# Attention outputs turned by DMA transposes of two f16 halves instead of fp32 TensorE transposes, from the second batch on

## The chip, the cores and the metric

One core of a Trainium2 chip runs the whole program. The metric is device microseconds of one execution. Engines are written as in the profile: PE is TensorE's matmul side and PEld its weight load, DVE is VectorE, ACT ScalarE, POOL GpSimd, and SP SyncE, which issues every DMA of this kernel.

## The reference

There are B = 8 batches of H = 8 heads, with S = 1152 keys and D = 64. Queries are averaged in pairs, so a head has TQ = 576 of them. The attention result, with the heads side by side, is the input x of a channel mix:

```python
q_pool = q.reshape(B, H, S // 2, 2, D).mean(axis=3)
scores = q_pool @ k.T / sqrt(D)
attn   = exp(scores - max);  attn /= attn.sum(-1) + 1e-9
x      = (attn @ v).transpose(0, 2, 1, 3).reshape(B, 576, 512)

x_prev = x shifted by one token, zeros first
xk, xr = mu_k * x + (1 - mu_k) * x_prev,  mu_r * x + (1 - mu_r) * x_prev
out    = sigmoid(xr @ w_r) * (relu(xk @ w_k) ** 2 @ w_v)
```

## The kernel before, in words

**Tiling.** The 64 heads are counted by n. Each is worked in six blocks of QN = 96 queries (`block`): first-pass scores (L479, nine matmuls of 128x96), a maximum over keys on DVE (L486), a small matmul that turns it (L489), a second maximum (L492), a small matmul that spreads it (L494), an ACT instruction that writes it into a row of the query tile (L497), second-pass scores (L503), and the exponential on ACT (L509), which leaves the packed weights `pf`. POOL takes their low parts out into `pl` (L512). Three PSUM tiles `s0` to `s2` rotate over the blocks. Keys and values of the next head are split into f16 pairs by `prep`: `kr` is loaded, ACT and POOL make `kn` (L430, L435), and a DMA transpose on SP's queue turns it into `ks1` (L438), nine blocks of 128x128 in one instruction. Queries of a pair of heads go the same way through `qn` (L397) and a DMA transpose to `qT` (L413).

**The place of the change.** `window` multiplies weights with values (L538, L540, L545) into the one PSUM tile `a`. A head has five windows, the first of 64 queries and four of 128. After the last of them ACT copies the first window's low part across (L562), DVE adds it (L564), and the result is divided into `xb` (L566 to L569), a single fp32 buffer of [128 queries, 5 windows, 2 heads, 64]. When the second head of a pair is there (hh = 1), five fp32 transposes on PE (L581), three and then two, turn `xb` by windows back into `a`, and ACT copies each part into `xt` (L584): `xt` is [128 features of the pair, 4 pairs, 1 + 576 tokens] in fp32, one of three buffers by batch. The transposes and the copies therefore stand between a pair and the next head's first window, which writes the same tile `a`. There are 32 pairs.

**The channel mix.** `ff` works tiles of 256 tokens, 18 in all, as soon as the batch that holds their last token is done. `mix` forms xk and xr from `xt` (ACT L653, DVE L656), rounds (ACT L662) and takes the rest on POOL (L664); the products are on PE (L684) with three f16 terms for each, ACT squares (L711, L713), POOL splits (L715), and so on to the output. Since a tile sums over all 512 features, it needs all four pairs of its batch. The three tiles that need batch 7 are left when attention ends; for the last batch the products take turns in five PSUM tiles, so that the first 8 of the 24 terms of each of four of them can run ahead.

**Weights.** `weights` loads 20 pieces through the two staging tiles `st0` and `st1` (4 KB a partition each) and splits them into f16 pairs on ACT, DVE and POOL; this is done while the first batches run.

**The order.** Nothing is issued when it is written. Every step is recorded by `op(engine, cost, function, r=, w=, key=)` with a cost in microseconds, what it reads and writes, and a key; `Issue.run` simulates several list schedules from these costs and fixed latencies, takes the one that comes out shortest, and issues every engine's instructions in that order. The order on each engine is then fixed; at run time an instruction waits only for the semaphores of what it needs, with everything behind it on its engine or queue. A cost in an `op` call is thus no work, but it moves the order. A step marked `port` (every POOL step, and a DVE step so marked) is kept apart from others so marked in the simulation.

Of the kernel before, what the change touches and what calls it, by code (L numbers as in the profile page):

```python
# [12 lines left out]
F16 = mybir.dt.float16  # L13
# [3 lines left out]
AF = mybir.ActivationFunctionType  # L17
# [3 lines left out]
P = 128  # L21
# [237 lines left out]
def kernel(  # L259
# [40 lines left out]
    def bufs(name, n, shape, dt):  # L300
        return [const.tile(shape, dt, name=f"{name}{i}") for i in range(n)]
# [43 lines left out]
    r32, tmp = bufs("r32", 2, [P, 2, T], F32), bufs("tmp", 2, [P, T], F32)  # L345
    ex, em = (bufs(n, 2, [P, DM], F32) for n in ("ex", "em"))
    st = bufs("st", 2, [P, 1024], I32)
    whi, wlo = {}, {}
    for n, w, kc in (("k", w_k, NG), ("v", w_v, NF), ("r", w_r, NG)):
        whi[n] = const.tile([P, kc, w.shape[1]], F16, name=f"w{n}_hi")  # L350
# [108 lines left out]
    def block(n, j, i, t):  # L459

        hp, z = n % 2, i % 3
        qi = n // 2 % 2
        q0 = hp * TQ + j * QN
        qhi, qlo = (qT[qi][:, r].rearrange("p j x -> p (j x)")[:, q0:q0 + QN] for r in (0, 1))
        kh, kl = ([(t_, qi, hp, j, j0) for j0, j1 in ((0, 5), (5, NQ)) if q0 < j1 * P and q0 + QN > j0 * P]
                  for t_ in ("qT", "qTl"))
        s = s_b[z]
        rows = slice(j * QN, (j + 1) * QN)
        mxz, mbz = mx[z], mb[z]

        def cols(c0, c1):
            return s[:, P + c0 * QN:P + c1 * QN]

        def grid(c0, c1):
            return cols(c0, c1).rearrange("p (c q) -> p c q", q=QN)

        def scores(c0, c1):
            for c in range(c0, c1):
                nc.tensor.matmul(cols(c, c + 1), ks1[hp][:, c, :], qhi,  # L479
                                 start=(c == c0), stop=False, skip_group_check=True)  # L480

        for c0, c1 in BK:
            op("PE", (c1 - c0) * 0.043, lambda c0=c0, c1=c1: scores(c0, c1),
               r=[("ks1", hp, c) for c in (0, 5) if c < c1 and (c0 < 5 or c)] + kh, w=[("s", z)], key=t)

        op("DVE", 0.967, lambda: nc.vector.tensor_reduce(mxz, grid(0, NC).rearrange("p c q -> p q c"),  # L486
                                                         axis=AX.X, op=ALU.max),
           r=[("s", z)], w=[("mx", z)], key=t)
        op("PE", 0.054, lambda: nc.tensor.matmul(s[0:QN, 0:P], mxz, identb, start=False, stop=False,  # L489
                                                 skip_group_check=True),  # L490
           r=[("mx", z)], w=[("s", z)], key=t + O_MAX)
        op("DVE", 0.199, lambda: nc.vector.tensor_reduce(mbz[0:QN], s[0:QN, 0:P], axis=AX.X, op=ALU.max),  # L492
           r=[("s", z)], w=[("mb", z)], key=t + O_MAX)
        op("PE", 0.05, lambda: nc.tensor.matmul(s[:, 0:QN], mbz[0:QN].broadcast_to([QN, P]),  # L494
                                                 negi[0:QN, 0:QN], start=False, stop=False, skip_group_check=True),
           r=[("mb", z)], w=[("s", z)], key=t + O_MAX)
        op("ACT", 0.133, lambda: nc.scalar.activation(qlo[QN:QN + 1], s[QN:QN + 1, 0:QN], AF.Prelu,  # L497
                                                      scale=1.0 - EPS, alpha=(1.0 + EPS) / (1.0 - EPS)),
           r=[("s", z)] + kl, w=kl, key=t + O_MAX)

        def scores2(c0, c1):
            for c in range(c0, c1):
                nc.tensor.matmul(cols(c, c + 1), ks2[hp][:, c, :], qlo,  # L503
                                 start=False, stop=True, skip_group_check=True)

        for c0, c1 in BK:
            op("PE", (c1 - c0) * 0.043, lambda c0=c0, c1=c1: scores2(c0, c1),
               r=[("ks2", hp)] + kl, w=[("s", z)], key=t + O_EXP)
        op("ACT", NC * QN / 1200 + 0.051, lambda: nc.scalar.activation(  # L509
            pf[:, :, HALF + rows.start:HALF + rows.stop], grid(0, NC), AF.Exp, bias=SHIFT, scale=0.125 / (2.0 * SQ)), r=[("s", z)], w=[("pf", j)], key=t + O_EXP)  # L510
        def lows(to, r0, r1, buf):
            op("POOL", NC * (r1 - r0) / 1000 + 0.066, lambda: nc.gpsimd.tensor_scalar(  # L512
                to, half(pf, U16, 0)[:, :, HALF + r0:HALF + r1], LO, 1.0, op0=ALU.mult, op1=ALU.mult),
               r=[("pf", j)], w=[buf], key=t + O_REST)

        r0 = rows.start
        if j == 0:
            lows(half(pf, F16, 1)[:, :, 0:HALF], 0, HALF, ("pside",))
            r0 = HALF
        lows(pl[:, :, r0:rows.stop], r0, rows.stop, ("pl", j))  # L520

    def window(n, w, t):


        b, h = divmod(n, H)
        g, hh = divmod(h, 2)
        r0, size, _ = WIN[w]
        side = size < P
        jv = n % NV
        VN = D + 1  # L530
        vk = [(x, jv, c0) for x in ("vt", "vtl") for c0 in (0, 5)]
        js = range(r0 // QN, (r0 + size - 1) // QN + 1)
        a0, rows = w * VN, slice(r0, r0 + P)
        his = slice(0, P) if side else slice(HALF + r0, HALF + r0 + P)

        def hi(c0, c1):
            for c in range(c0, c1):
                nc.tensor.matmul(a_b[:, a0:a0 + VN], half(pf, F16, 1)[:, c, his], vt[jv][:, c, D:D + VN],  # L538
                                 start=(w == 0 and c == 0), stop=False, skip_group_check=True)
                nc.tensor.matmul(a_b[:, a0:a0 + D], half(pf, F16, 1)[:, c, his], vt[jv][:, c, 0:D],  # L540
                                 start=False, stop=(side and c == NC - 1), skip_group_check=True)

        def lo(c0, c1):
            for c in range(c0, c1):
                nc.tensor.matmul(a_b[:, a0:a0 + VN], pl[:, c, rows], vb[jv][:, c, 0:VN],  # L545
                                 start=False, stop=(c == NC - 1), skip_group_check=True)

        for c0 in (0, 3, 6):
            op("PE", 3 * 0.0595, lambda c0=c0: hi(c0, c0 + 3),
               r=vk + [("pf", j) for j in js] + ([("pside",)] if side else []) + ([("a",)] if c0 or w else []),  # L550
               w=[("a",)], key=t)
        for c0, c1 in () if side else ((0, 5), (5, NC)):
            op("PE", (c1 - c0) * 0.030, lambda c0=c0, c1=c1: lo(c0, c1),
               r=[("vb", jv)] + [("pl", j) for j in js] + [("a",)], w=[("a",)], key=t)
        if w < NW - 1:
            return

        u = a_b[:, 0:NW * VN].rearrange("p (k x) -> p k x", k=NW)
        z = n % 2
        dz, xz = den[z], xb[0]  # L560
        up = slice(HALF, P)
        op("ACT", 0.25, lambda: nc.scalar.activation(cross[up], a_b[0:HALF, 0:VN], AF.Copy, scale=VLO),  # L562
           r=[("a",)], w=[("cross",)], key=t + O_EVAC)
        op("DVE", 0.16, lambda: nc.vector.tensor_tensor(a_b[up, 0:VN], a_b[up, 0:VN], cross[up], op=ALU.add),  # L564
           r=[("cross",), ("a",)], w=[("a",)], key=t + O_EVAC)
        op("DVE", 0.075, lambda: nc.vector.tensor_scalar(dz, u[:, :, D], GUARD, None, op0=ALU.add),  # L566
           r=[("a",)], w=[("den", z)], key=t + O_EVAC)
        op("DVE", 0.08, lambda: nc.vector.reciprocal(dz, dz), r=[("den", z)], w=[("den", z)], key=t + O_EVAC)
        op("DVE", 0.07 + NW * D / 960, lambda: nc.vector.tensor_tensor(  # L569
            xz[:, :, hh], u[:, :, 0:D], dz.unsqueeze(2).broadcast_to([P, NW, D]), op=ALU.mult),  # L570
           r=[("den", z), ("a",)], w=[("xb", hh)], key=t + O_EVAC)
        if hh == 0:
            return
        for k0, k1 in TURN:
            q0, qe = spans(k0, k1)
            base = qe - (k1 - k0) * P

            def turned(k0=k0, k1=k1, base=base):
                for k_ in range(k0, k1):
                    r_ = WIN[k_][0] + WIN[k_][1] - P - base  # L580
                    nc.tensor.transpose(a_b[:, r_:r_ + P], xz[:, k_].rearrange("p h d -> p (h d)"), ident)  # L581

            op("PE", 0.11 * (k1 - k0), turned, r=[("xb", 0), ("xb", 1)], w=[("a",)], key=t + O_TURN)
            op("ACT", 0.051 + (qe - q0) / 1200, lambda q0=q0, qe=qe, base=base: nc.scalar.copy(  # L584
                xt[b % 3][:, g, 1 + q0:1 + qe], a_b[:, q0 - base:qe - base]),
               r=[("a",)], w=[("xt", b % 3, g, k0)], key=t + O_TURN)
# [233 lines left out]
```

## Time and profile before

| | |
|---|---|
| median of 3 runs | 1158.41 us (1158.35 to 1158.62) |
| the profiled execution | 1158.5 us, span 1156.7 us |
| granted TensorE clock, mean | 0.988 |
| PE, PEld | 1105.0, 916.0 us |
| DVE, ACT, POOL | 859.4, 875.9, 740.0 us |
| DMA share of the span, queue 1 | 47.1% |

The span is the time from the first to the last instruction in the trace; the execution's own time is 1.8 us longer. The rows are busy time: of an engine with instructions that overlap, it is the time in which at least one runs. Busy shares are averages; the stages differ, and a change is judged in the stage in which it lies.

### The profile page before, as it was taken

To read this page: it belongs to the slowest core of one execution; us is meant where nothing else is said; L and a number is where in the kernel's file an instruction comes from. 1 tells how busy PE (TensorE), PEld (TensorE's weight loads), DVE (VectorE), ACT (ScalarE), POOL (GpSimd) and SP (SyncE) were. 2 spreads that over 40 slices of the span, in tenths; PEclk is the share of its full clock that TensorE was granted. 3 is DMA by queue.
4 is the path that set the end of the run, shared out by engine and by line. 5 is a ranking of instruction groups with operands and counts; after the bars stand their busy time and mean duration, and the time that the engine had idled before them with its cause. 6 is when DMAs were issued, how large, how long until landed. Compare 5 with 4: busy or idle time off the path is not lost.

```text
span 1156.7 us, 44885 instructions
## 1 busy us (share of the span) xinstructions
PE 1105.0 (96%) x18928; PEld 916.0 (79%) x18928; DVE 859.4 (74%) x1622; ACT 875.9 (76%) x1810; POOL 740.0 (64%) x883
## 2 busy tenths in 40 slices
PE   3878889999999999999999999999999999999998
PEld 3767787988889887978788888879797878887565
DVE  6899987888887777787687878777787778673320
ACT  4778888788778787887878786978887788775643
POOL 3767786766767567666767675857666676654431
PEclk9799999999999999999999999999999999999999
DMA  9687655466354644565444444655544444310000
GB/s 225 183 201 183 172 137 138 99 130 133 99 124 104 126 90 111 124 114 115 93 118 97 116 96 110 119 116 102 114 109 104 111 96 93 73 27 11 19 20 28
DMA packets 222378, 126.64 MB, mean 109 GB/s; under 512 B 157664, under 2 KB 194528, under 8 KB 222176
## 3 DMA queue, kind: packets, MB, share of 16 engines
q1 hardware_dynamic: 222176, 123.77, 47.1%
q8 instruction: 148, 2.42, 0.9%
q14 instruction: 54, 0.44, 0.1%
HBM read 67.11 MB, written 9.44 MB: 66 GB/s over the span
## 4 chain that ended last, share of the span: by engine, by line
PE 85%; DVE 5%; ACT 4%; DMA 3%; issue 2%; SPq 1%; ACTq 0%; DVEq 0%
PE f L684 33%; PE s L479 11%; PE s L503 11%; PE a L538 7%; PE a L540 7%; PE a L545 6%; PE s L684 4%; ACT pf L509 2%; DVE mx L486 2%; PE s L489 2%; PE a L684 2%; PE s L494 1%; PE a L581 1%; DMA ks<-kn 1%; DMA kr<-in_k_dram 1%
## 5 line engine op out<-in xcount | busy, mean ns | idle before, releaser
L486 DVE TENSOR_REDUCE mx<-s 128x96 f16<-128x864 f32 x384 | 401.5, 1054 | 107.2 <-PE s L479 59.8
L512 POOL TENSOR_SCALAR pl<-pf 128x864 f16<-128x864 uint16 (+1 forms) x384 | 337.8, 880 | 186.3 <-ACT pf L509 157.9
L509 ACT ACTIVATE pf<-s 128x864 int32<-128x864 f32 x384 | 337.6, 889 | 84.6 <-PE s L503 50.5
L479 PE MATMUL s<-qT,ks 128*128 128x96 f16 x3456 | 217.8, 208 | 25.6 <-ACT pf L509 12.7
L538 PE MATMUL a<-vt,pf 128*128 128x65 f16 x2880 | 230.2, 194 | 1.5 <-ACT pf L509 0.9
L540 PE MATMUL a<-vt,pf 128*128 128x64 f16 x2880 | 230.4, 194 | 0.0
L479 PEld LDWEIGHTS <-ks 128*128 128x128 f16 x3456 | 185.4, 99 | 51.3 <-issue 18.4
L503 PE MATMUL s<-qT,ks 128*128 128x96 f16 x3456 | 215.0, 208 | 7.5 <-ACT qT L497 6.8
L538 PEld LDWEIGHTS <-pf 128*128 128x128 f16 x2880 | 200.5, 99 | 6.3 <-ACT pf L509 1.2
L503 PEld LDWEIGHTS <-ks 128*128 128x128 f16 x3456 | 181.9, 99 | 28.7 <-issue 9.1
L540 PEld LDWEIGHTS <-pf 128*128 128x128 f16 x2880 | 192.4, 98 | 7.7 <-issue 1.0
L492 DVE TENSOR_REDUCE mb<-s 96x1 f16<-96x128 f32 x384 | 109.3, 285 | 79.9 <-PE s L489 71.8
L497 ACT ACTIVATE qT<-s 1x96 f16<-1x96 f32 x384 | 92.1, 242 | 88.4 <-PE s L494 75.7
L684 PE MATMUL f<-xhk,wk_hi 128*128 128x256 f16 x496 | 135.1, 272 | 0.2
L684 PE MATMUL f<-xlk,wk_hi 128*128 128x256 f16 x496 | 135.1, 272 | 0.0
L684 PE MATMUL f<-xhk,wk_lo 128*128 128x256 f16 x496 | 135.1, 272 | 0.0
L545 PE MATMUL a<-vb,pl 128*128 128x65 f16 x2304 | 124.0, 194 | 0.2 <-POOL pl L512 0.2
L684 PEld LDWEIGHTS <-wk_hi 128*128 128x128 f16 x1152 | 107.0, 98 | 11.0 <-issue 0.4
L435 POOL TENSOR_TENSOR kn<-kr,kn 128x320 f16<-128x320 f32 x126 | 99.6, 802 | 17.5 <-ACT kn L430 13.5
L715 POOL TENSOR_TENSOR gl<-g 128x512 f16<-128x512 f32 x72 | 77.3, 1075 | 46.1 <-ACT g L713 43.8
L545 PEld LDWEIGHTS <-pl 128*128 128x128 f16 x2304 | 99.2, 98 | 5.1 <-POOL pl L512 0.5
L489 PE MATMUL s<-identb,mx 128*96 128x128 f16 x384 | 87.6, 228 | 6.8 <-DVE mx L486 6.7
(96 smaller groups left out, 2089.9 us busy)
## 6 DMA issues: line engine op xcount, KB each, us to landing
kr<-in_k_dram SPq DMA_DIRECT2D x64, 288.0 KB, 3.0
vr<-in_v_dram SPq DMA_DIRECT2D x64, 288.0 KB, 3.2
qr<-in_q_dram SPq DMA_DIRECT2D x32, 320.0 KB, 3.4
ks<-ks SPq DMA_DIRECT2D x64, 144.0 KB, 2.5
out_dram<-em SPq DMA_DIRECT2D x36, 256.0 KB, 2.4
qr<-in_q_dram SPq DMA_DIRECT2D x32, 256.0 KB, 3.3
st<-in_moe_w_k_dram SPq DMA_DIRECT2D x8, 512.0 KB, 4.9
st<-in_moe_w_v_dram SPq DMA_DIRECT2D x8, 512.0 KB, 4.6
```

The source lines that it names most:

```text
L435: lambda cs=cs, en=nc.vector if ve else nc.gpsimd: en.tensor_tensor(kn[i][:, cs, D:P], kr[i][:, cs], kn[i][:, cs, 0:D], op=ALU.subtract),
L479: nc.tensor.matmul(cols(c, c + 1), ks1[hp][:, c, :], qhi, start=(c == c0), stop=False, skip_group_check=True)
L486: op("DVE", 0.967, lambda: nc.vector.tensor_reduce(mxz, grid(0, NC).rearrange("p c q -> p q c"), axis=AX.X, op=ALU.max), r=[("s", z)], w=[ ...
L489: op("PE", 0.054, lambda: nc.tensor.matmul(s[0:QN, 0:P], mxz, identb, start=False, stop=False, skip_group_check=True), r=[("mx", z)], w=[( ...
L492: op("DVE", 0.199, lambda: nc.vector.tensor_reduce(mbz[0:QN], s[0:QN, 0:P], axis=AX.X, op=ALU.max), r=[("s", z)], w=[("mb", z)], key=t + O ...
L503: nc.tensor.matmul(cols(c, c + 1), ks2[hp][:, c, :], qlo, start=False, stop=True, skip_group_check=True)
L509: op("ACT", NC * QN / 1200 + 0.051, lambda: nc.scalar.activation(pf[:, :, HALF + rows.start:HALF + rows.stop], grid(0, NC), AF.Exp, bias=S ...
L512: op("POOL", NC * (r1 - r0) / 1000 + 0.066, lambda: nc.gpsimd.tensor_scalar(to, half(pf, U16, 0)[:, :, HALF + r0:HALF + r1], LO, 1.0, op0= ...
L538: nc.tensor.matmul(a_b[:, a0:a0 + VN], half(pf, F16, 1)[:, c, his], vt[jv][:, c, D:D + VN], start=(w == 0 and c == 0), stop=False, skip_gr ...
L540: nc.tensor.matmul(a_b[:, a0:a0 + D], half(pf, F16, 1)[:, c, his], vt[jv][:, c, 0:D], start=False, stop=(side and c == NC - 1), skip_group ...
L545: nc.tensor.matmul(a_b[:, a0:a0 + VN], pl[:, c, rows], vb[jv][:, c, 0:VN], start=False, stop=(c == NC - 1), skip_group_check=True)
L684: nc.tensor.matmul(ps, terms[i][0], terms[i][1], start=(first and i == 0), stop=(i == last), skip_group_check=True)
```

## The change

For heads n >= 8, that is for the last 28 of the 32 pairs, the PE transposes and the two ACT copies are replaced. ACT rounds the whole `xb` (640 elements a partition) to f16 (`xbh`), POOL subtracts to get the rest in f16 (`xbl`), two DMA transposes on SP's queue turn each of them (five blocks of 128x128 each) into `xth` and `xtl`, and POOL adds the two into `xt` in fp32 (576 elements). The four f16 arrays lie in the staging tiles: `xbh` and `xbl` in `st0`, `xth` and `xtl` in `st1`. The first four pairs are turned as before. Beside this the costs that the order is planned with are raised for three steps that are not changed themselves.

```diff
+    xbh, xbl, xth, xtl = (st[i].bitcast(F16)[:, o * NW * P:(o + 1) * NW * P] for i in (0, 1) for o in (0, 1))
+    old = [[(m, i) for m in ("st", "sl")] for i in (0, 1)]
...
-        op("ACT", 0.133, lambda: nc.scalar.activation(qlo[QN:QN + 1], s[QN:QN + 1, 0:QN], AF.Prelu,
+        op("ACT", 0.36, lambda: nc.scalar.activation(qlo[QN:QN + 1], s[QN:QN + 1, 0:QN], AF.Prelu,
...
-        op("ACT", 0.25, lambda: nc.scalar.activation(cross[up], a_b[0:HALF, 0:VN], AF.Copy, scale=VLO),
+        op("ACT", 0.34, lambda: nc.scalar.activation(cross[up], a_b[0:HALF, 0:VN], AF.Copy, scale=VLO),
...
-        op("DVE", 0.16, lambda: nc.vector.tensor_tensor(a_b[up, 0:VN], a_b[up, 0:VN], cross[up], op=ALU.add),
+        op("DVE", 0.36, lambda: nc.vector.tensor_tensor(a_b[up, 0:VN], a_b[up, 0:VN], cross[up], op=ALU.add),
...
         if hh == 0:
             return
+        if n >= H:
+            flat = "p k h d -> p (k h d)"
+            op("ACT", 0.63, lambda: nc.scalar.copy(xbh, xz.rearrange(flat)),
+               r=[("xb", 0), ("xb", 1)], w=[("xbh",), *old[0]], key=t + O_TURN)
+            op("POOL", NW * P * 0.0019 + 0.09, lambda: nc.gpsimd.tensor_tensor(xbl, xz.rearrange(flat), xbh, op=ALU.subtract),
+               r=[("xb", 0), ("xb", 1), ("xbh",)], w=[("xbl",), *old[0]], key=t + O_TURN)
+            for kx, x, to in (("xbh", xbh, xth), ("xbl", xbl, xtl)):
+                op("DMA", 0.8, lambda x=x, to=to: nc.sync.dma_start_transpose(to.rearrange("p (k x) -> p k x", k=NW), x),
+                   r=[(kx,)], w=[(kx, "t"), *old[1]], key=t + O_TURN, tail=2.0)
+            op("POOL", TQ * 0.0019 + 0.09, lambda: nc.gpsimd.tensor_tensor(
+                xt[b % 3][:, g, 1:1 + TQ], xth[:, HALF:], xtl[:, HALF:], op=ALU.add),
+               r=[("xbh", "t"), ("xbl", "t")], w=[("xt", b % 3, g, k0) for k0, k1 in TURN], key=t + O_TURN, port=True)
+            return
         for k0, k1 in TURN:
```

## The prediction

> **What bounds the kernel now.** I read the page first: busy times, then the chain that ended last.
>
> ```profile
> span 1156.7 us, 44885 instructions
> ...
> PE 1105.0 (96%) x18928; PEld 916.0 (79%) x18928; DVE 859.4 (74%) x1622; ACT 875.9 (76%) x1810; POOL 740.0 (64%) x883
> ...
> PE 85%; DVE 5%; ACT 4%; DMA 3%; issue 2%; SPq 1%; ACTq 0%; DVEq 0%
> PE f L684 33%; PE s L479 11%; PE s L503 11%; PE a L538 7%; PE a L540 7%; PE a L545 6%; PE s L684 4%; ACT pf L509 2%; DVE mx L486 2%; PE s L489 2%; PE a L684 2%; PE s L494 1%; PE a L581 1%; DMA ks<-kn 1%; DMA kr<-in_k_dram 1%
> ```
>
> PE holds 85% of the chain, and L581, the transposes that the change removes, has its own place there. An average can hide stages, so next come stretches of time: busy us of PE, PEld, DVE, ACT and POOL, the granted clock, the DMA share.
>
> ```profile
> 30.00:145.00 115.00, 92.20 (x1865) 82.84 (x1864) 104.35 (x196) 89.38 (x181) 83.74 (x96) 0.90 0.74 186
> 145.00:290.00 145.00, 141.38 (x2541) 119.86 (x2538) 120.82 (x230) 119.36 (x249) 101.53 (x121) 1.00 0.55 126
> 290.00:435.00 145.00, 144.32 (x2604) 122.55 (x2601) 114.18 (x217) 117.12 (x245) 99.00 (x120) 1.00 0.50 110
> 860.00:1000.00 140.00, 139.09 (x2501) 116.72 (x2498) 105.64 (x199) 112.28 (x236) 97.63 (x116) 1.00 0.46 103
> 1060.00:1075.00 15.00, 15.00 (x124) 9.34 (x121) 5.22 (x14) 6.33 (x17) 2.13 (x3) 1.00 0.05 19
> ```
>
> From 290 us on PE idles 0.7 of 145 us and 0.9 of 140, at full clock. In 30 to 145, where the weights are split, it idles 22.8 of 115; the first four pairs, unchanged, lie mostly there. No other engine passes 84% after 145 us: ACT and DVE have some 20% left in 290:435, POOL 46 us of 145.
>
> Busy PE could still be matmuls that wait inside. So I looked at starts in PE's timeline around the last pair, and at PE's waits between 200 and 1060 us:
>
> ```profile
> 1068.23 0.38 PE L684 MATMUL f<-wr_hi,xlr 128*128 128x512 f16 x1
> 1068.44 0.49 PE L581 MATMUL a<-ident,xb 128*128 128x128 f32 x3
> 1068.77 0.38 PE L684 MATMUL f<-wr_hi,xr 128*128 128x512 f16 x1
> ...
> 1070.07 0.38 PE L581 MATMUL a<-ident,xb 128*128 128x128 f32 x2
> 1070.28 0.38 PE L684 MATMUL f<-wr_hi,xr 128*128 128x512 f16 x1
> ```
>
> ```profile
> PE s L494 <- DVE mb L492: 1.1, 3, 0.5
> PE f L684 <- ACT em L734: 1.0, 3, 0.5
> PE s L479 <- ACT pf L509: 0.7, 1, 0.7
> PE a L538 <- ACT xt L584: 0.4, 1, 0.4
> PE f L684 <- ACT r L711: 0.4, 1, 0.4
> ```
>
> The next matmul starts 0.33 us after the first of three transposes and 0.21 us after the first of two: 0.109 us apiece, with neighbours closed up on both sides. The waits sum to 3.6 us in 860. PE's instruction stream is the bound wherever the 28 changed pairs lie, and what leaves that stream comes off the end.
>
> **The change, part by part.** The durations of its pieces come from these groups and, for one row, from the line's own view (min/median/max):
>
> ```profile
> L581 PE MATMUL a<-ident,xb 128*128 128x128 f32 x160 | 29.4, 283 | 0.5 <-ACT xt L584 0.4
> L584 ACT COPY xt<-a 128x320 f32<-128x320 f32 x32 | 13.7, 427 | 5.5 <-PE a L581 5.1
> L584 ACT COPY xt<-a 128x256 f32<-128x256 f32 x32 | 11.9, 372 | 0.8 <-PE a L581 0.5
> L397 ACT ACTIVATE qn<-qs 128x640 f16<-128x640 f32 x32 | 23.4, 732 | 1.7 <-DVE qs L394 1.4
> L715 POOL TENSOR_TENSOR gl<-g 128x512 f16<-128x512 f32 x72 | 77.3, 1075 | 46.1 <-ACT g L713 43.8
> L435 POOL TENSOR_TENSOR kn<-kr,kn 128x320 f16<-128x320 f32 x63 | 54.1, 859 | 15.0 <-ACT kn L430 12.6
> L435 POOL TENSOR_TENSOR kn<-kr,kn 128x256 f16<-128x256 f32 x63 | 46.9, 745 | 2.4 <-ACT kn L430 0.9
> ```
>
> *Transposes removed.* 28 pairs x (0.33 + 0.21) = 15.1 us of PE's stream. Bounds: L581's 1% of the chain, read as at least 0.5%, is 5.8 us for all pairs, a floor the closed starts argue against; its whole busy time, 29.4 x 28/32 = 25.7 us, is too much, since 283 ns of one overlaps its neighbours. I take 15.1, from the starts.
>
> *ACT.* Off: 427 + 372 = 799 ns. On: a 640-element rounding, 732 ns as L397. Over 28 pairs that is -1.9 us on an engine that PE hardly waits for: 0. The next head's first window no longer waits for copies out of `a`; that wait is the 0.4 us row above, so also 0.
>
> *POOL.* The subtraction has 640 elements, f16 from fp32. From L435, 114 ns for 64 more elements, it would be 859 + 570 = 1.43 us; from L715, 1075 x 640/512 = 1.34. I take 1.35. No row has the addition of two f16 into fp32; by L715's rate 576 elements are 1.21. Together 2.56 us a pair, 72 us in all: POOL goes from 740 to 812 us, in a stretch such as 860:1000, with four pairs at the mean pace, from 97.6 to about 108 of 140. It stays below PE, so on the path it costs nothing as long as its results come before PE wants them. How far ahead they are, one example in the timeline shows, POOL's last low parts `pl` and then PE's matmuls that read them:
>
> ```profile
> 1057.67 1.90 POOL L512 TENSOR_SCALAR pl<-pf 128x864 f16<-128x864 uint16 x2 [1.44 <-ACT pf L509]
> ```
>
> ```profile
> 1064.90 0.45 PE L545 MATMUL a<-vb,pl 128*128 128x65 f16 x9
> ```
>
> They end at 1059.57, 5.3 us early.
>
> *SP's queue.* Two more transposes a pair wait there, the first for ACT, the second for POOL's subtraction; behind them stand the next heads' loads, the `ks` and `qT` transposes and the output stores. Issue takes about as long as L438's 1.3 us, for nine blocks where the new ones have five (the rows are from the line's own view, the list of DMA issues with the time to landing, and PE's waits over the whole span):
>
> ```profile
> L438 SPq DMA_TRANSPOSE ks<-kn x64: 1257/1317/2781, 8.3 to 1021.9; - x64
> ...
> ks<-kn SPq DMA_TRANSPOSE x64, 3.4
> ...
> PE s L479 <- DMA ks<-kn: 11.6, 1, 11.6
> ```
>
> 56 x 1.32 = 74 us of queue time at most. PE waited for a `ks` transpose once in 64 heads, the 11.6 us of the start. Landing takes 3.4 us; the DMA engines are half idle. A second transpose held 1.4 us by POOL delays what is behind it by that: 0 on the path, with the `ks` lead as cover; without it, up to 1.4 us a pair, 39 us.
>
> *The last pair.* Here no attention is left to hide the longer way, so I walked it.
>
> ```profile
> 1067.29 0.49 DVE L569 TENSOR_TENSOR xb<-a,den 128x320 f32<-128x320 f32 x1
> ...
> 1068.97 0.43 ACT L584 COPY xt<-a 128x320 f32<-128x320 f32 x1 [3.36 <-PE a L581]
> ...
> 1071.24 0.67 POOL L664 TENSOR_TENSOR xlk<-xk,xhk 128x256 f16<-128x256 f32 x1 [11.67 <-ACT xhk L662]
> ...
> 1078.08 0.27 PE L684 MATMUL s<-xlk,wk_hi 128*128 128x256 f16 x1
> ```
>
> Before, `xb` is done at 1067.78, the first part of `xt` at 1069.40, 1.6 us on, and the last `xlk` at 1071.91; PE, filled with tile 14's products, resumes tile 15's first product at 1078.08. That is 6.2 us of cover. After: rounding 0.73, subtraction 1.35, landing 3.4, addition 1.21, hand-offs some 0.1 each: 7.1 us from `xb` to `xt`, 5.5 more than now. The cover holds: 0; without it 5.5 us.
>
> *The raised plan costs and new queueing.* The order is planned anew on every engine. Today's waits of 3.6 us show how well a plan fits; on a slightly fuller POOL and SP I add 1.5 us. Bounds: 3.6 us won back at the best, and 8 us lost, a third of the 22.8 us that PE idles in the early stretch, which the new plan also shuffles.
>
> Sum against the profiled execution (1158.5 us: span 1156.7 and 1.8 around it): 1158.5 - 15.1 + 1.5 = 1144.9. The median of the runs is 0.1 lower, so 1144.8.
>
> **The rivals.**
>
> *POOL takes part of it back.* The DVE line that mixes xk and reads only SBUF operands, while POOL is often at work, shows what that can do:
>
> ```profile
> L656 DVE SCALAR_TENSOR_TENSOR xk<-xt,mu_k,tmp x96: 270/474/1310, 92.9 to 1101.4; 128x256 f32<-128x256 f32 x48, 128x64 f32<-128x64 f32 x16, 128x192 f32<-128x192 f32 x16, 128x128 f32<-128x128 f32 x16
> ```
>
> At worst it is over twice its median. If the 72 us of new POOL time hold DVE up one for one in a tenth of it, and PE with it, 7 us go: 1152. Against: PE waits for DVE hardly at all (1.1 us above), and DVE has 34 us of 140 free. Chance 0.09. The Trainium skill, page "SBUF — State Buffer", section "Who interferes with whom", has this as a lock: a DVE instruction with two SBUF inputs and a GpSimd one that reads SBUF exclude each other for a whole instruction. The spread of L656 agrees; it gives no other sum.
>
> *The last pair is late.* If a landing takes longer, or the new plan has spent tile 14's products by then, PE stands still in the tail for up to the 5.5 us of the longer way: 1150. For it: the longest L438 issue took 2781 ns, over twice the median. Against: the cover is 0.7 us longer than the way, and the plan knows the way. Chance 0.06. The Trainium skill, page "VectorE: DVE Perf Modes", section "The three transpose paths", speaks against the change here: it gives a 128x128 16-bit transpose as 1309 ns by DMA and 390 ns on TensorE, and its rules prefer TensorE where a PSUM destination will do. Ten blocks one after another would by that be an estimated 13.1 us, 8.3 more than the 1.35 + 3.4 above, and the sum about 1152.4; nine blocks landing in 3.4 us in this trace do not bear that out.
>
> *PE was not full.* If PE's stream had slack inside the busy time, or the holes closed up no more than other waits opened, nothing would be seen: 1158. The Trainium skill, page "Perfetto Trace Analysis", section "Identifying the Most-Contended Engine", warns that matmul busy time is a bad measure and points to LDWEIGHTS; its 79% here would leave a fifth free. The starts, 0.11 us apart in the transposes and 0.21 behind a 512-column product, with no gap between the two kinds, speak against slack. Chance 0.06.
>
> *Slower: POOL stuck behind a landing.* POOL's addition stands in a fixed order and waits for both transposes; behind it stand low parts `pl` for L545 and splits for L684. If the plan expects the landing too early, POOL stands still for up to 3.4 us a pair. It decides from 15.1/28 = 0.54 us of PE a pair. With 5.3 us of lead in the one example, most would be swallowed; if a fifth comes through, 0.7 us x 28 = 19.6, the time is 1163. Chance 0.10.
>
> *The new plan gains too.* If it also wins the 3.6 us and some of the 22.8, the time is below 1140. Chance 0.03.
>
> **How the numbers follow.** The forecast has 0.66, with an own range of 1139.5 (the 3.6 us won back: 1158.4 - 15.1 - 3.6 = 1139.7) to 1149 (1 us of reading error in the 15.1, and 4.5 us lost to the plan: 1158.4 - 14.1 + 4.5 = 1148.8). Reaching over the first two rivals gives 1139 to 1152; left out are slower and no change (0.16) and the outermost of the rest (0.04). A difference of 0.2%, 2.3 us, is about what a measurement of this kernel can tell from none. Faster: 0.66 + 0.09 + 0.06 + 0.03 = 0.84; same 0.06; slower 0.10.
>
> **What would show it.** L581 at 20 instructions instead of 160, PE busy near 1090 us, still over 99% in stretches past 290 us; POOL near 812 us; new transposes landing in at most 3.4 us; PE's waits in the middle below 8 us; the last pair's `xt` about 7 us after `xb` with PE not idle. It is wrong if PE's idle time in the middle grows by over 5 us, if PE waits for `pl` or `ks`, or if PE idles in the tail before tile 15.

## The result, and the profile after

The changed kernel takes 1149.67 us (median of 4 runs, 1148.93 to 1149.96); the kernel before took 1158.51 beside it (median of 4). The ratio is 0.9917, 95% interval 0.9900 to 0.9935: faster, by 8.8 us where 13.6 were forecast. The profiled execution took 1149.55 us, with a span of 1147.8.

The page of the changed kernel, busy times and the chain that ended last by engine:

```profile
span 1147.8 us, 44731 instructions
...
PE 1094.7 (95%) x18788; PEld 906.6 (79%) x18788; DVE 881.8 (77%) x1622; ACT 881.4 (77%) x1782; POOL 817.5 (71%) x939
...
PE 86%; DVE 7%; ACT 2%; issue 2%; DMA 2%; POOL 1%; SPq 0%; ACTq 0%; DVEq 0%; POOLq 0%
```

PE lost 140 matmuls and 10.3 us of busy time, 5 less than the forecast's 15.1 for those 140. POOL gained 77.5 us, and DVE 22.4 us although none of its work changed. The same stretches of time as before, with the columns PE, PEld, DVE, ACT, POOL, granted clock, DMA share and GB/s:

```profile
30.00:145.00 115.00, 95.09 (x1880) 86.37 (x1879) 105.34 (x194) 89.19 (x179) 82.63 (x95) 0.84 0.81 185
145.00:290.00 145.00, 137.89 (x2508) 116.42 (x2508) 120.60 (x217) 115.71 (x234) 110.17 (x125) 0.98 0.62 127
290.00:435.00 145.00, 142.68 (x2585) 120.62 (x2582) 118.76 (x225) 118.33 (x244) 109.81 (x127) 1.00 0.62 125
860.00:1000.00 140.00, 139.82 (x2510) 116.05 (x2507) 112.24 (x208) 114.68 (x236) 107.82 (x124) 1.00 0.52 111
```

From 290 us on the picture is nearly that of before: PE idles 2.3 us instead of 0.7 in the third row, and 0.2 instead of 0.9 in the fourth. What differs more is the granted clock of the first two rows: 0.84 where it was 0.90, and 0.98 where it was 1.00. Over the whole run it is 0.981 against 0.988, and (1 - clock) x span is the time that the missing clock is worth if PE is always the bound: 21.8 us now, 13.9 before. The difference, 7.9 us, is about what is missing, and it arises before the first new instruction runs, at 188.6 us.

The new steps, in groups (line, engine, operation, shapes, count, busy us, mean ns), the DMA transposes with their time to landing, and PE's waits between 200 and 1050 us:

```profile
L580 POOL TENSOR_TENSOR st<-xb,st 128x640 f16<-128x640 f32 x28 | 41.7, 1490 | 15.0 <-ACT st L578 13.9
L585 POOL TENSOR_TENSOR xt<-st 128x576 f32<-128x576 f16 x28 | 37.6, 1343 | 7.8 <-DMA st<-st 6.6
L578 ACT CAST st<-xb 128x640 f16<-128x640 f32 x28 | 20.2, 723 | 3.8 <-DVE xb L571 3.4
```

```profile
L583 SPq DMA_TRANSPOSE st<-st x56: 1199/1234/2421, 190.7 to 1059.2; - x56
...
DMA to landing us min/median/max: 2.5/2.8/5.6
```

```profile
PE s L481 <- ACT pf L511: 1.8, 5, 0.5
PE s L491 <- DVE mx L488: 1.0, 3, 0.3
PE a L540 <- POOL vb L454: 0.6, 1, 0.6
...
PE f L699 <- ACT r L726: 0.2, 1, 0.2
```

POOL's two steps take 2.83 us a pair, and the addition stood waiting for a landing twice, 6.6 us in all. PE's eight rows of waits sum to 5.2 us, only 0.6 of it for POOL. So the new steps are hidden, as far as one trace can say.

### The profile page after: what moved, and what is told of

It reads as the page before. It is cut to its first block, busy times and chain, and to the rows that moved or that the text cites. A ratio compares the mean times of both kernels' runs of the same rounds, so it can differ in the third digit from the quotient of the medians.

```text
span 1147.8 us, 44731 instructions
## 1 busy us (share of the span) xinstructions
PE 1094.7 (95%) x18788; PEld 906.6 (79%) x18788; DVE 881.8 (77%) x1622; ACT 881.4 (77%) x1782; POOL 817.5 (71%) x939
## 4 chain that ended last, share of the span: by engine, by line
PE 86%; DVE 7%; ACT 2%; issue 2%; DMA 2%; POOL 1%; SPq 0%; ACTq 0%; DVEq 0%; POOLq 0%
PE f L699 34%; PE s L481 12%; PE s L505 11%; PE a L540 7%; PE a L542 7%; PE a L547 6%; PE s L699 4%; DVE mx L488 3%; PE s L491 2%; PE a L699 2%; ACT pf L511 1%; PE s L496 1%; DVE vt L451 1%; DVE mb L494 1%; DMA qT<-qn 1%
## 5 line engine op out<-in xcount | busy, mean ns | idle before, releaser
L540 PE MATMUL a<-vt,pf 128*128 128x65 f16 x2880 | 234.5, 194 | 1.1 <-POOL vb L454 0.6
L542 PE MATMUL a<-vt,pf 128*128 128x64 f16 x2880 | 234.7, 194 | 0.1
L540 PEld LDWEIGHTS <-pf 128*128 128x128 f16 x2880 | 202.4, 99 | 4.8 <-issue 0.2
L505 PEld LDWEIGHTS <-ks 128*128 128x128 f16 x3456 | 182.5, 100 | 22.4 <-issue 5.3
L542 PEld LDWEIGHTS <-pf 128*128 128x128 f16 x2880 | 194.5, 98 | 6.6 <-issue 1.7
L437 POOL TENSOR_TENSOR kn<-kr,kn 128x320 f16<-128x320 f32 x126 | 96.7, 775 | 14.0 <-ACT kn L432 8.8
```

What stands on the lines that cost most here:

```text
L437: lambda cs=cs, en=nc.vector if ve else nc.gpsimd: en.tensor_tensor(kn[i][:, cs, D:P], kr[i][:, cs], kn[i][:, cs, 0:D], op=ALU.subtract),
L505: nc.tensor.matmul(cols(c, c + 1), ks2[hp][:, c, :], qlo, start=False, stop=True, skip_group_check=True)
```

## The experiments

Two theories were to be told apart. **A:** the order of the early stretch, planned anew, leaves PE's clock lower, and that ate the missing time. **B:** the new steps on POOL and SP's queue ate it. "Half clock" in the expectations is twice the missing clock: 0.988 over 1157 us is some 27 to 28 us at half clock.

**Only the costs.** The kernel before, with the three raised plan costs:

```diff
-        op("ACT", 0.133, lambda: nc.scalar.activation(qlo[QN:QN + 1], ...
+        op("ACT", 0.36, lambda: nc.scalar.activation(qlo[QN:QN + 1], ...
-        op("ACT", 0.25, lambda: nc.scalar.activation(cross[up], ...
+        op("ACT", 0.34, lambda: nc.scalar.activation(cross[up], ...
-        op("DVE", 0.16, lambda: nc.vector.tensor_tensor(a_b[up, 0:VN], ...
+        op("DVE", 0.36, lambda: nc.vector.tensor_tensor(a_b[up, 0:VN], ...
```

> The kernel before with only the three raised plan costs; no instruction is added or removed, only the order is planned anew. Of the 15 us that left TensorE's stream some 6 did not reach the end; in the changed kernel the first 180 us show about 17 us more at half clock, and TensorE's idle time from 145 to 290 us went from 3.6 to 7.1 us. Theory A (the new order in the early stretch, brought by the raised costs, ate them): about 1163 to 1164 us, five over before, with the half-clock time in the first 180 us grown as in the changed kernel. Theory B (the new steps on GpSimd and the DMA queue ate them): 1157 to 1160 us, clock mean near 0.988.

1167.2 us (1164.8 to 1171.1), ratio to before 1.0067 (1.0049 to 1.0084). No work differs (the counts of instructions by engine are those of before), and it is 8 us slower, even more than A said. Its stretch from 30 to 180 us, then that of the changed kernel, then that of the kernel before:

```profile
30.00:180.00 150.00, 124.58 (x2284) 112.43 (x2283) 131.92 (x243) 113.74 (x226) 102.99 (x119) 0.83 0.67 167
```

```profile
30.00:180.00 150.00, 124.60 (x2378) 112.53 (x2377) 135.68 (x247) 114.89 (x231) 108.23 (x125) 0.86 0.75 169
```

```profile
30.00:180.00 150.00, 124.41 (x2481) 112.42 (x2480) 133.34 (x251) 117.22 (x239) 111.10 (x128) 0.92 0.69 170
```

The columns are as above. PE is busy for about 124.5 us and idle for about 25.5 in all three, but at clocks of 0.83, 0.86 and 0.92, and it gets through 2284, 2378 and 2481 matmuls. The page of this kernel, whose profiled execution had a span of 1167.9 us, shows the same for the whole run:

```profile
PE 1115.1 (95%) x18928; PEld 925.2 (79%) x18928; DVE 869.4 (74%) x1622; ACT 877.4 (75%) x1810; POOL 733.8 (63%) x883
```

PE idles 52.8 us (1167.9 less 1115.1), against 51.7 before (1156.7 less 1105.0), but the same 18928 matmuls keep it busy 10.1 us longer. So of the 11.2 us that lie between the two spans 10.1 are lost in slower matmuls and only 1.1 in waits; the missing clock of these two executions, 25.7 against 13.9 us, differs by 11.8.

**Only the turning.** The changed kernel with the three costs put back (the diff above, reversed).

> The new way of turning with the three plan costs left as they were. Theory A: 1143 to 1145 us, the whole 15 us with the usual 1 us lost. Theory B: 1149 to 1150 us, as the changed kernel.

1150.3 us (1149.2 to 1151.9), ratio 0.9919 (0.9905 to 0.9933): the number that B gave, and A in the form "the raised costs did it" falls. But the clock is again 0.980 to 0.983. Both edits, each alone, lower the clock.

**No turning.** The changed kernel with one ACT copy of the outputs in place of the new steps, which leaves the turning out:

```diff
+            op("ACT", 0.6, lambda: nc.scalar.copy(
+                xt[b % 3][:, g, 1:1 + TQ], xz.rearrange("p k h d -> p (k h d)")[:, HALF:]),
+               r=[("xb", 0), ("xb", 1)], w=[("xt", b % 3, g, k0) for k0, k1 in TURN], key=t + O_TURN)
```

> The changed kernel, but from the second batch on one ScalarE copy writes the outputs unturned: the turning is left out, and with it the f16 halves, the GpSimd steps and the DMA transposes. Theory A: still about 1149 us, since the raised costs and an order planned anew stay. Theory B: 1142 to 1144 us, and VectorE's busy time back from 882 to about 860 us.

1141.6 us (1141.2 to 1142.1), ratio 0.9844 (0.9831 to 0.9856), 0.4 us below what B said; on its page DVE is back, as B said too:

```profile
PE 1089.3 (96%) x18788; PEld 900.6 (79%) x18788; DVE 858.2 (75%) x1622; ACT 876.4 (77%) x1782; POOL 740.7 (65%) x883
```

Yet its clock is also back, at 0.988, so it does not tell the two apart by its time alone. Without the missing clock it takes 1127.7 us, and the changed kernel 1127.9 (table below): with the new steps or without, the same to within the 1.2 us to which the clock is given.

**Other draws.** The order is chosen by simulated schedules whose durations and delays are drawn at random. The changed kernel, its order chosen with other draws:

```diff
-        trials = [times(LATE, SLACK, 1 + i) for i in range(3)]
+        trials = [times(LATE, SLACK, 11 + i) for i in range(3)]
```

> The changed kernel with other random draws for the three trial schedules among which the order is chosen (11 to 13 instead of 1 to 3); same instructions, another order. Theory A in the form that any new order moves the early stretch by some us: the time moves by 2 to 6 us either way from 1149.7. Theory B: within 1.5 us of 1149.7.

1143.9 us (1140.5 to 1144.5), ratio 0.9853 (0.9836 to 0.9871). The same instructions in another order are 5.7 us faster, at a clock of 0.985: A in its second form, against B.

**The early order put back.** In the changed kernel the order of before is computed as well, and everything that it has ahead of the second `xb` of pair 5 (the tenth head) is issued in that order; the swap does the reverse.

```diff
-                order = sorted(range(N), key=lambda n: (start[n], n))
+                order = sorted(range(N), key=lambda n: (lead.get(n, N), start[n], n))
...
+    order = old_.run(WAIT)
+    early = [names[0][i] for i in order]
+    early = early[:early.index("seam")]
+    for i in new.run(WAIT, first=[at[x] for x in early]):
+        new.ops[i][2]()
```

> The changed kernel, but up to the end of the tenth head every engine gets its instructions in the order of the kernel before; the rest is planned as in the changed kernel. The runs so far fit one line: time = a constant of the kernel + half of the time at half clock in the first 170 us (27 us before, 44 changed). Theory A (the early order decides the half-clock time, and that ate the 6 us): half clock near 27 us and 1140 to 1143 us. Theory B (the new steps or their places in the later order ate them): 1148 to 1151 us.

1144.5 us (1143.7 to 1146.0), ratio 0.9872 (0.9858 to 0.9887), clock 0.988: the clock came back with the order, as A said, and some 5 of the 6 us; B's 1148 is out. It misses A's range by 1.5 us: behind the seam, from 180 to 400 us, PE idles 5.2 us instead of the changed kernel's 2.6 (214.80 and 217.37 busy of 220). Its stretch from 30 to 180 us has a clock of 0.93, and in 123.7 us of busy time, 0.9 less than in the changed kernel, 114 more matmuls (their kinds are not quite the same):

```profile
30.00:180.00 150.00, 123.66 (x2492) 111.68 (x2491) 134.06 (x253) 118.19 (x242) 111.65 (x128) 0.93 0.70 172
```

> The swap: the kernel before, its first ten heads in the order of the changed kernel, the rest planned as before. It has none of the new steps. Theory A: half clock near 44 us and 1165 to 1168 us. Theory B: 1157 to 1160 us.

1164.0 us (1161.6 to 1166.4), ratio 1.0035 (1.0024 to 1.0047), clock 0.984. The kernel before, which has none of the new steps, gets slower when its first ten heads run in the changed kernel's order. That is A's direction and not B's, a little short of A's size: the clock fell to 0.984, not to 0.981.

**The kernel before, other draws.** The same edit of the draws as above.

> The kernel before with the other draws (11 to 13): no instruction differs, only the order. Theory A: 1158.5 + half of (half-clock time in the first 170 us - 27.2), within 2 us, wherever that lands; a spread of some 5 us between draws is expected. Theory B: within 1.5 us of 1158.5.

1159.7 us (1158.2 to 1162.6), ratio 1.0001 (0.9991 to 1.0011), clock 0.988. The clock is that of before and so is the time: it fits A's line, but the spread that I expected is not there, and B holds here too.

**PE kept busy early.** In the changed kernel each block of the first ten heads gets eight matmuls without use:

```diff
+    nc.vector.memset(a_b[:, 384:512], 0.0)
...
+        if n < H + 2:
+            def fill():
+                for _ in range(8):
+                    nc.tensor.matmul(a_b[:, 384:512], identb, identb, start=False, stop=False, skip_group_check=True)
+
+            op("PE", 0.43, fill, r=[("s", z)], key=t)
```

> The changed kernel with eight idle 128x128 f16 matmuls added in each block of the first ten heads, behind its first scores (60 x some 0.43 us = 26 us of TensorE, most of it where it idles anyway; the product goes to unused columns and is not read). Theory A, with TensorE's waits as what lowers the clock: half-clock time falls from 44 to below 20 us and the time to 1136 to 1146 us, added work and all. If the half clock only goes along with the waits and costs nothing by itself: 1150 to 1165 us, since work is added.

1153.0 us (1151.3 to 1156.7, six runs; a seventh is told of at the end), ratio 0.9943 (0.9928 to 0.9959), clock 0.993. The clock did what A says: the missing clock falls from 21.8 to 8.1 us. The time did not: it lies where it was expected if the half clock cost nothing by itself. At full clock the kernel now takes 1144.9 us, 17 more, so most of the added work (26 us by its plan cost) would not have fallen into holes; the only trace of this kernel is of the seventh run, so where it fell is not shown. By its time alone this run therefore decides nothing; that the lost clock costs time by itself rests on the kernel with only the costs, above. What it shows is that more matmuls on PE early raise the clock, and that this is no way to win the time back.

**The clock in the plan.** The order is chosen from more schedules, with a fine for windows in which PE is idle, once for each kernel:

```diff
-PLANS = ((0.08, 0.1), (0.12, 0.15))
+PLANS = ((0.08, 0.1), (0.12, 0.15), (0.05, 0.08), (0.1, 0.2), (0.16, 0.12))
...
+            for x in busy[6:int(until / win)]:
+                total += win / 2 if half else 0.0
+                half = x / win < 0.62
...
-                total = sum(self.follow(eng, d, p, s, order, port)[1] for d, p, s in trials) / len(trials)
+                total = 0.0
+                for d, p, s in trials:
+                    at, end = self.follow(eng, d, p, s, order, port)
+                    total += (end + self.slow(eng, d, at)) / len(trials)
```

> The changed kernel, its order chosen among more schedules (five slack settings, ten rounds) with a fine: for each 3.4 us window of the first 200 us in which TensorE would be busy under 62%, half a window is added to the schedule's length, since the traces show the clock halved in the next window behind such ones. If that rule is the cause, half-clock time is below 30 us and the time 1138 to 1143 us, the fastest so far. If the clock is no matter of such windows and orders differ by luck, half-clock time is anywhere from 25 to 45 us and the time 1141 to 1151 us.

1141.9 us (1139.0 to 1142.8), ratio 0.9836 (0.9813 to 0.9858): the fastest complete version here and faster than both kernels, though its interval overlaps that of the other draws. The time lies within what the rule gave, but also within what luck gave, and so does the half clock, some 30 us. The clock is 0.986 in the profile, 0.987 at the median of the runs.

> The kernel before with the same fine in the choice of its order. By the rule: half-clock time under 27 us and 1153 to 1158 us; the distance to the changed kernel chosen in the same way is then what the turning is worth at equal clock, 15 to 18 us. By luck alone: 1157 to 1165 us.

1164.7 us (1161.1 to 1166.9), ratio 1.0037 (1.0024 to 1.0050), clock 0.985: a miss for the rule on both counts, and within what luck gave. The distance to the changed kernel chosen in the same way is 22.8 us, 21.4 without the missing clock, where 15 to 18 were expected. The fine counts windows in a simulated schedule, and that the chip's windows fall elsewhere is a guess. So that the fine is what made the other one fast is not shown; more schedules to choose from, and luck, would do as well.

All kernels side by side: the median time, the clock, the time that the missing clock is worth, (1 - clock) x span, and what is left without it, each the median over a kernel's runs (the clock is given to 0.001, which is 1.2 us).

| kernel | us | clock | missing clock, us | rest, us |
|---|---|---|---|---|
| before (20 runs beside four of the experiments) | 1159.6 | 0.987 | 15.0 | 1145.4 |
| only the costs | 1167.2 | 0.981 | 22.7 | 1145.0 |
| before, early order as changed | 1164.0 | 0.984 | 18.6 | 1145.1 |
| before, other draws | 1159.7 | 0.988 | 13.9 | 1145.8 |
| before, clock in the plan | 1164.7 | 0.985 | 17.4 | 1147.5 |
| changed | 1149.7 | 0.981 | 21.8 | 1127.9 |
| only the turning | 1150.3 | 0.982 | 21.2 | 1129.3 |
| changed, other draws | 1143.9 | 0.985 | 17.1 | 1126.9 |
| changed, early order as before | 1144.5 | 0.988 | 13.7 | 1130.8 |
| changed, clock in the plan | 1141.9 | 0.987 | 14.8 | 1126.1 |
| no turning | 1141.6 | 0.988 | 13.7 | 1127.7 |
| changed, early filled | 1153.0 | 0.993 | 8.1 | 1144.9 |

The kernel before ran beside the other six experiments too, 28 times, with a rest of 1145.4 and 1146.4 us. The last column falls into two groups. Everything with the old turning stands at 1145.0 to 1147.5, everything without those PE transposes at 1126.1 to 1130.8, except the filled one, which had work added. The change is worth some 17.5 us at equal clock, and the order that came with it cost some 7 of them. Both are no sharper than the column: kernels with the same new steps spread over 4.7 us in it.

How the order does that, windows of 3.4 us show. First the changed kernel, then the kernel before:

```profile
144.50:147.90 3.40, 1.62 (x29) 1.25 (x27) 3.31 (x8) 3.03 (x7) 3.08 (x5) 1.00 0.42 128
147.90:151.30 3.40, 2.87 (x34) 2.60 (x31) 2.99 (x6) 1.69 (x5) 1.39 (x3) 0.51 0.45 87
...
161.60:165.00 3.40, 1.77 (x23) 1.18 (x23) 3.40 (x7) 3.06 (x7) 2.59 (x4) 1.00 0.45 87
165.00:168.40 3.40, 3.40 (x29) 2.76 (x29) 3.30 (x9) 2.72 (x5) 2.61 (x4) 0.50 0.31 94
```

```profile
128.40:131.80 3.40, 1.80 (x25) 1.29 (x26) 3.28 (x9) 3.28 (x7) 2.65 (x4) 1.00 0.64 204
131.80:135.20 3.40, 3.40 (x58) 3.40 (x58) 2.53 (x6) 1.97 (x5) 1.84 (x3) 0.51 0.33 128
```

In each pair of rows PE is idle for about half of a window at full clock, and the next window is granted half. DVE, which splits weights between its reductions there, is nearly full in the first row of each. PE's waits in the changed kernel's window from 144.5 to 147.9 us are two short ones:

```profile
PE s L491 <- DVE mx L488: 0.9, 1, 0.9
PE s L481 <- ACT pf L511: 0.9, 1, 0.9
```

All 13 falls of the clock between 20 and 170 us in these two traces stand behind a window in which PE was busy at most 66%; the changed kernel has nine of them, the kernel before four. The reverse holds less sharply: in this stretch of the two traces every window at full clock with PE busy up to 59% lost the next one, but in the trace of before one at 61% (70.4 to 73.8 us) did not, and in that of the kernel without turning one at 54% (70.4 to 73.8 us) did not. Counted by windows, the changed kernel spends 13 at half clock and the kernel before 8; at 1.7 us lost in each that is 22 and 14 us, the missing clock of the table over again. The total idle time of that stretch is the same, 25.4 us from 30 to 180 us against 25.6 before. It is bunched otherwise. The Trainium skill, page "TensorE: Matmul & The Clock Gate", section "Why this matters for your kernels", tells to avoid idle gaps of TensorE over some 3 us, since one idle window halves the clock. The trace agrees on the window and on the half, but two gaps of 0.9 us in one window were enough here.

## Why the prediction was right or wrong

The time lies in the stated range, just above the forecast's own range of 1139.5 to 1149, and the mechanism was right. One term of the sum was mis-sized.

- *Transposes removed, 15.1 us.* At equal clock 17.5 (1145.4 - 1127.9). The 2.4 us more are not taken apart. The kernel without turning has them as well (1127.7), which points to what was removed, but they are less than the 4.7 us by which orders differ in that column.
- *ACT, 0.* 723 ns were 732 in the forecast; POOL's subtraction waited for it, 13.9 us in all, but PE never did.
- *POOL, 72 us, 0 on the path.* 79.3 us, since 1490 and 1343 ns stand for 1350 and 1210. DVE took 22.4 us more, and without the new steps its time was back at 858.2: the hold-up that the first rival had, though most of it, 14.6 us, lies in the line that makes `vt` and not in the xk line that the prediction looked at. Yet PE's wait for DVE in the middle stayed at 1.7 us, and the rest of 1127.9 equals that without the new steps, 1127.7: 0 on the path holds.
- *SP's queue, 0.* Landing took 2.8 us in the middle case against 3.4. PE did not wait for a `ks` transpose but for the one at the start. The sign "landing in at most 3.4 us" was missed: the longest took 5.6.
- *The last pair, 0.* The way is there, a little longer than forecast, in the timeline of the changed kernel:

```profile
1054.94 0.49 DVE L571 TENSOR_TENSOR xb<-a,den 128x320 f32<-128x320 f32 x1
```

```profile
1056.27 1.40 POOL L580 TENSOR_TENSOR st<-xb,st 128x640 f16<-128x640 f32 x1 [4.13 <-ACT st L578]
1061.98 1.27 POOL L585 TENSOR_TENSOR xt<-st 128x576 f32<-128x576 f16 x1 [4.31 <-DMA st<-st]
```

  From `xb` (1055.43) to `xt` (1063.25) are 7.8 us, 7.1 forecast. SP's queue held the second transpose until 1059.25, behind an output store, though its input was there at 1057.67. PE had other products meanwhile: from 1060 to 1100 us it is busy 40.00 of 40, so the cover held.
- *The raised plan costs and new queueing, 1.5 us, at most 8.* This is the term that failed: 6.8 to 7.9 us (missing clock now less missing clock before, 21.8 against 15.0 or 13.9), nearly its upper bound. I took the plan's risk for waits of PE, and for those the 1.5 us was about right: from 200 to 1050 us PE idles 6.2 us against 4.7 before, though with 98.4% in 290:435 it missed the "over 99%". And I read the early stretch only as a place where PE idles anyway. What the runs showed instead is that the bunching of that idle time sets the clock, and that a new plan shuffles it. The profile of before had it in view: a clock of 0.90 in 30:145, the only stretch with less than 1.00 among those quoted, and I passed over it.

That the time is in the range is in part luck. The two errors, 2.4 us more gained and some 5 to 6 more lost, offset each other in part, and the range reached up to 1152 only for two rivals that did not come; the clock was in none of its terms.

Of the rivals, POOL's part, the late last pair and the stuck POOL did not come; PE was full, as the 17.5 us show, so weight loads at 79% of the span were no room to spare in this kernel. Why these orders bunch PE's idle time as they do is open: raised costs alone do it, the new steps alone do it, and other draws undo it in part.

## What to carry to other kernels

When an order is planned by a program, every edit, even of a cost, is two edits: measure the new work and the new order apart, by draws or by holding a part of the order fixed. Put the granted clock into the sum: (1 - clock) x span, taken off each run, brought kernels with the same work together here whose times lay up to 8 us apart. Idle time on PE ahead of the stretch where it is full is not free, if enough of it falls into one window of 3.4 us.

## What the runs showed of the hardware

The clock moved in steps of 3.4 us between full and half, and in these traces one half-idle step was mostly enough to lose the next. More surprising was one run of seven of the early-filled kernel, at 1875 us. Its profile, with the columns as above:

```profile
50.00:70.00 20.00, 19.93 (x293) 19.72 (x291) 12.02 (x21) 10.30 (x22) 10.00 (x13) 0.54 0.43 131
400.00:1050.00 650.00, 649.02 (x6860) 495.42 (x6859) 305.31 (x584) 319.42 (x644) 289.42 (x341) 0.56 0.32 73
```

With PE busy almost without a gap the clock stayed near half from 18 us to the end; it never came back. It is 0.56 in single windows of 3.4 us too (600.0 to 603.4, for one), so here it is no mix of full and half ones. The other six runs of the same kernel had 0.992 to 0.994, and no run of another kernel did this. The cause is open and was not tried. A DMA transpose of five blocks of 128x128 landed 2.8 us after its issue and one of nine after 3.4 (medians): four blocks more cost 0.6 us, so most of that time is not paid by the block.
